# All heads of the second attention chunk score by two passes over exact halves

## The chip, the cores and the metric

The program runs on one core of one Trainium2 chip. Its time is device time in microseconds (us), the median of several runs. The core has a matrix engine (TensorE; PE in the profile, with its weight loads as PEld), a vector engine (VectorE, DVE), an activation engine (ScalarE, ACT), GpSimd (POOL) and a queue engine (SyncE, SP) that issues nearly all transfers. Each engine takes its own instructions in the order in which they are written down, and waits at an instruction until what it needs is there.

## The reference

The inputs are q, k and v (4 batches, 8 heads, 576 positions, 64 wide) and the weights of two feed-forward layers. All is float32.

```
scores = (q @ k^T) / sqrt(64)
scores = scores - slope[h] * |i - j|      where 0 <= i - j < 128, else -1e9
attn   = softmax(scores);  out = attn @ v
x  = out, heads side by side              # 2304 tokens x 512
x  = (silu(x @ w_gate) * (x @ w_val)) @ w_out        # 512 -> 1536 -> 512
h  = x @ w_in                                         # 512 -> 2048
y  = (h * tanh(softplus(h))) @ w_out2                 # 2048 -> 512
```

## The kernel before

The 2304 tokens are cut into five chunks (512, 384, 512, 512 and 384 tokens). For each chunk the kernel computes attention and then the first feed-forward layer; the second layer follows for all tokens. Chunk 0's attention stands alone at the start. From then on the two kinds of work are interleaved: while PE runs the feed-forward groups of one chunk, the attention of the next chunk is handed out in pieces between them. So the attention of the second chunk (chunk 1, the one that changes) lies among the feed-forward groups of chunk 0.

**Two ways to score a head.** `s_full(h)` (line 143) decides by the table `S_FULL` (line 28): in the first `S_FULL[ci]` pairs of heads of chunk `ci` the scores are plain float32 products, in the others they are made of halves. In the trace a plain product appears as `s_ps<-k,q`, two records per product. For the halves, `split` (line 190) makes three tiles of a head:

```
nc.scalar.activation(out=Q, in_=q, func=AF.Copy, scale=c)      # L203, ACT
hi_act(K1, k)                                                  # L123, ACT
nc.vector.scalar_tensor_tensor(out=Q[64:128], in0=q[64:128], ...)   # L205, DVE
lo_dve(KL, k, K1)                                              # L126, DVE
```

`Q` holds the rounded query on partitions 0 to 63 and what rounding left over on 64 to 127; `K1` holds the rounded key twice, `KL` its remainder twice. `score` (line 211) then runs two products per block, `s_ps<-K,Q` and `s_ps<-KL,Q`, with 128 instead of 64 rows of contraction. A plain pair needs one load of q and k for both heads (lines 165 and 166) and one scaling on ACT (L195). A head of halves needs its q and k twice, on both halves of the partitions (lines 173 and 174), and the scratch tiles `qraw`, `kraw`, `Q`, `K1` and `KL` exist once each, so that the load of one head waits for the split of the head before it.

**Scores of one head of chunk 1.** Its 384 tokens are four blocks of 64, 128, 128 and 64 queries, in two PSUM banks; each bank is one piece of work (`s_piece`, line 344), with a cost: 1.7 where the head is plain, 0.87 where it is made of halves. After the second bank the head is normalized (`norm`: L257, L260 on DVE, L264 on ACT), later transposed (`t_ps`, L271 on PE), masked on POOL and multiplied with v (`o_ps`).

**What sets the order.** PE's order is written out by hand: after each feed-forward group the loop hands out attention pieces until their share of the summed cost has caught up with the groups done. The order on DVE, ACT, POOL and SP is made by a scheduler when the kernel is built.

**What else DVE does there.** During chunk 0 the weights of the first layer arrive as 64-bit numbers and are converted: five steps on ACT and DVE (L434, L439, L446, L451, L460), then a split (`w<-cw,w`, L126). Feed-forward groups are `g_ps<-xt,w` (12 matmuls a group, 24 for one of twelve blocks) and `acc<-h,ringf` (8 records), with L686 on ACT and L687 and L697 on DVE behind them.

Of the kernel before, what the change touches and what calls it, by code (L numbers as in the profile page):

```python
# [24 lines left out]
PLAIN = 3  # L25
CT = DM // 128
A_CHUNKS = [512, 384, 512, 512, 384]
S_FULL = [4, 2, 0, 0, 0]
TB = 384
NPB = NT // (2 * TB)  # L30
NJ = NF2 // 2
# [62 lines left out]
def body(ctx: ExitStack, tc: tile.TileContext, qT, kT, vP, w1, w1o, w2, cst, yT):  # L94
# [903 lines left out]
    with tc.manual_schedule(engines={mybir.EngineType.PE}):  # L998
# [19 lines left out]
        bpool["a"] = ap0  # L1018
        atts = [attention(app, p, ci, S_FULL[ci], ci == 0) for ci, p in enumerate(plansA)]
        pieces = attention_pieces(atts)  # L1020
# [166 lines left out]
```

## Time and profile before

| | |
|---|---|
| median of 3 runs | 941.0 us (940.25 to 941.48) |
| the profiled execution's own time | 941.18 us |
| its span, first to last instruction | 939.4 us |
| busy: PE, PEld | 916.6 us (98%), 819.3 us (87%) |
| busy: DVE, ACT, POOL | 699.1 us (74%), 518.7 us (55%), 202.3 us (22%) |
| plain scores of chunk 1 | 32 records from 53.2 to 95.4 us |
| scores of chunk 1 from halves | 16 + 16 records from 109.8 to 144.1 us |

The profile is of one execution. Times in it count from the span's start. A row of the timeline gives the start, the duration, the engine, the line, the operation, the tiles (written <- read), a count, and in brackets how long the engine had stood idle and for whom. The end of a matmul is modelled, and neighbours overlap a little; the time from one start to the next start is the surer measure, on DVE and ACT too.

### The profile page before, as it was taken

What the parts mean: (1) busy time and instruction counts of PE and PEld (TensorE: products, weight loads), DVE (VectorE), ACT (ScalarE), POOL (GpSimd) and SP (SyncE); (2) the same over time, 40 slices, a digit from 0 to 9 for tenths busy, and PEclk for the clock granted to TensorE, in tenths of its full rate; (3) what the DMA queues carried; (4) which work ended last, traced back from release to release, by engine and by line L of the source; (5) the groups of instructions that cost most, each with busy time, mean ns of one, the idle gap of its engine ahead of it and who ended that gap; (6) DMA issues with size and microseconds to landing.
All of it is one profiled execution on the core that took longest, in us unless ns stands there. A gap on an engine that the chain in (4) does not pass through costs nothing. (4 is left out here: it accounts for less than half of the span.)

```text
span 939.4 us, 14535 instructions
## 1 busy us (share of the span) xinstructions
PE 916.6 (98%) x5016; PEld 819.3 (87%) x5016; DVE 699.1 (74%) x1333; ACT 518.7 (55%) x1127; POOL 202.3 (22%) x332
## 2 busy tenths in 40 slices
PE   5999999999999999999999999999999999999998
PEld 4755678899988888888888999999999999999998
DVE  6898996677866776477665896688976689766874
ACT  6765667666575755355433554555535646355442
POOL 1312132110310332001012455452013410121000
PEclk8899999999999999999999999999999999999999
DMA  9855433366646554164527986526793257930375
GB/s 347 269 242 173 153 117 106 102 220 201 198 112 192 184 181 153 32 208 156 162 97 267 382 292 210 224 85 209 250 300 119 68 191 259 301 122 3 105 260 196
DMA packets 76729, 174.86 MB, mean 186 GB/s; under 512 B 8944, under 2 KB 52336, under 8 KB 66928
## 3 DMA queue, kind: packets, MB, share of 16 engines
q1 hardware_dynamic: 76512, 173.67, 56.1%
q8 instruction: 40, 0.66, 0.3%
q14 instruction: 33, 0.27, 0.1%
q10 hardware_dynamic: 144, 0.26, 0.1%
HBM read 138.25 MB, written 35.65 MB: 185 GB/s over the span
## 5 line engine op out<-in xcount | busy, mean ns | idle before, releaser
L116 PE MATMUL g_ps<-xt,w 128*128 128x512 f32 (+1 forms) x1440 | 318.3, 373 | 0.0
L116 PEld LDWEIGHTS g_ps<-xt,w 128*128 128x128 f32 x1440 | 257.6, 188 | 36.7 <-issue 3.5
L116 PE MATMUL bk<-op,wout 128*128 128x384 f32 x1008 | 176.2, 334 | 2.1 <-DMA wout<-w2o 2.0
L116 PEld LDWEIGHTS bk<-op,wout 128*128 128x128 f32 x1008 | 174.7, 188 | 3.2 <-ACT op L123 1.6
L116 PE MATMUL bk<-xs,win 128*128 128x384 f32 x1008 | 175.8, 334 | 0.7 <-DVE G L759 0.5
L116 PEld LDWEIGHTS bk<-xs,win 128*128 128x128 f32 x1008 | 174.7, 188 | 1.4 <-DVE G L759 0.8
L116 PE MATMUL acc<-hh,ring 128*128 128x512 f32 (+1 forms) x432 | 132.3, 369 | 0.0
L123 ACT ACTIVATE op<-G 128x768 fp32r<-128x768 f32 x84 | 71.2, 848 | 64.1 <-PE bk L116 53.6
L280 POOL TENSOR_SCALAR_AFFINE_SELECT PT<-PT 128x256 f32<-128x256 f32 (+4 forms) x80 | 44.4, 570 | 230.3 <-ACT PT L277 230.1
L126 DVE TENSOR_TENSOR op<-G,op 128x768 fp32r<-128x768 f32 x84 | 80.0, 964 | 16.1 <-ACT op L123 15.4
L116 PEld LDWEIGHTS acc<-hh,ring 128*128 128x128 f32 x432 | 80.0, 188 | 9.8 <-ACT hh L123 0.4
L851 POOL TENSOR_TENSOR t<-w 128x256 f32<-128x256 f32 x48 | 42.0, 897 | 206.9 <-issue 110.7
L116 PE MATMUL acc<-hl,ring 128*128 128x512 f32 (+1 forms) x216 | 79.0, 366 | 0.0
L249 ACT ACTIVATE Pt<-Pt,sm 128x128 f32<-128x128 f32 (+1 forms) x160 | 62.6, 393 | 14.1 <-DVE sm L245 13.6
L759 DVE TENSOR_TENSOR G<-u,bk 128x384 f32<-128x384 f32 x72 | 39.7, 553 | 40.0 <-PE bk L116 38.5
L686 ACT ACTIVATE t<-g_ps 128x512 f32<-128x512 f32 (+1 forms) x60 | 32.9, 549 | 47.3 <-PE g_ps L116 47.3
L1131 ACT ACTIVATE G<-G 128x384 f32<-128x384 f32 x72 | 37.3, 518 | 37.4 <-DVE G L759 37.4
L123 ACT ACTIVATE hh<-t 128x512 fp32r<-128x512 f32 (+1 forms) x54 | 31.3, 579 | 44.4 <-DVE t L702 44.2
L687 DVE SCALAR_TENSOR_TENSOR t<-t,g_ps 128x512 f32<-128x512 f32 (+1 forms) x60 | 37.6, 628 | 23.2 <-ACT t L686 23.1
L264 ACT ACTIVATE Pt<-Pt,sm 128x128 f32<-128x128 f32 (+1 forms) x144 | 46.5, 393 | 9.8 <-DVE sm L260 9.5
L126 DVE TENSOR_TENSOR hl<-t,hh 128x512 fp32r<-128x512 f32 (+1 forms) x54 | 36.5, 677 | 16.0 <-ACT hh L123 15.2
L702 DVE SCALAR_TENSOR_TENSOR t<-t,g_ps 128x512 f32<-128x512 f32 (+1 forms) x54 | 33.7, 624 | 19.2 <-PE g_ps L116 18.0
(84 smaller groups left out, 1268.1 us busy)
## 6 DMA issues: line engine op xcount, KB each, us to landing
wout<-w2o SPq DMA_DIRECT2D x42, 1024.0 KB, 7.0
wraw<-w SPq DMA_DIRECT2D x16, 1024.0 KB, 5.3
w2o<-chl SPq DMA_DIRECT2D x16, 896.0 KB, 8.2
wst<-w SPq DMA_DIRECT2D x12, 1024.0 KB, 8.0
cw<-w1od SPq DMA_DIRECT2D x24, 512.0 KB, 4.5
w<-w2d SPq DMA_DIRECT2D x24, 512.0 KB, 3.5
w2d<-cw SPq DMA_DIRECT2D x16, 512.0 KB, 4.6
wraw<-w1o SPq DMA_DIRECT2D x6, 1024.0 KB, 6.8
```

The lines of the kernel that those rows point to most:

```text
L116: nc.tensor.matmul(out=out, lhsT=lhsT, rhs=rhs, start=start, stop=stop, skip_group_check=True)
L123: return nc.scalar.activation(out=out, in_=in_, func=AF.Copy)
L126: return nc.vector.tensor_tensor(out=out, in0=in_, in1=hi.bitcast(F32), op=ALU.subtract)
L249: last_of["sum"] = nc.scalar.activation(out=Pt[:q.qn], in_=Pt[:q.qn], func=AF.Exp, scale=-1.0, bias=sm[:q.qn, i:i + 1], accum_out=sm[:q.qn ...
L264: last_of["exp"] = nc.scalar.activation(out=pt, in_=pt, func=AF.Copy, scale=r)
L280: nc.gpsimd.affine_select(out=here, in_=prev, pattern=[[0, m], [1, n]], compare_op=ALU.is_ge, fill=0.0, base=0, channel_multiplier=-1,)
L686: tanhs.append(nc.scalar.activation(out=t[:, :n], in_=st["g"][:, :n], func=AF.Tanh, scale=0.5))
L687: nc.vector.scalar_tensor_tensor(out=t[:, :n], in0=t[:, :n], scalar=1.0, in1=st["g"][:, :n], op0=ALU.add, op1=ALU.mult)
L702: nc.vector.scalar_tensor_tensor(out=t[:, :n], in0=t[:, :n], scalar=0.5, in1=vps[:, :n], op0=ALU.mult, op1=ALU.mult)
L759: last_of["add"] = nc.vector.tensor_tensor(out=out, in0=a, in1=b, op=op)
L851: nc.gpsimd.tensor_tensor(out=x[:, o], in0=a, in1=b, op=ALU.subtract)
L1131: last_of["mish"] = nc.scalar.activation(out=out, in_=in_, func=AF.Mish)
```

## The change

The second entry of the table goes from 2 to 0. Heads 0 to 3 of chunk 1 are then loaded, split and scored as heads 4 to 7 are already.

```
-S_FULL = [4, 2, 0, 0, 0]
+S_FULL = [4, 0, 0, 0, 0]
```

Since the cost of their score pieces falls from 1.7 to 0.87, the pieces of chunk 1 are also handed out at other places. The first place is PE's order from the first scores of chunk 1 on (s_ps are scores, g_ps the gate and value products, o_ps attention times v, acc the output products). Before:

```order
L116 MATMUL s_ps<-k_389,q_388 128x256
L116 MATMUL s_ps<-k_389,q_388 64x192
L116 MATMUL g_ps<-xt,w 128x512 x6
L116 MATMUL s_ps<-k_389,q_388 64x192
L116 MATMUL s_ps<-k_389,q_388 128x128
L116 MATMUL g_ps<-xt,w 128x512 x6
L116 MATMUL s_ps<-k_389,q_388 128x256
L116 MATMUL s_ps<-k_389,q_388 64x192
L116 MATMUL g_ps<-xt,w 128x512 x12
```

The same place in the changed kernel, from the second bank of head 0 (K_453) to the first bank of head 1 (K_646) and what follows:

```order
L116 MATMUL s_ps<-K_453,Q 128x128
L116 MATMUL s_ps<-KL,Q 128x128
L116 MATMUL g_ps<-xt,w 128x512 x3
L116 MATMUL s_ps<-K_646,Q 128x256
L116 MATMUL s_ps<-KL,Q 128x256
L116 MATMUL s_ps<-K_646,Q 64x192
L116 MATMUL s_ps<-KL,Q 64x192
L116 MATMUL g_ps<-xt,w 128x512 x3
L116 MATMUL s_ps<-K_646,Q 64x192
L116 MATMUL s_ps<-KL,Q 64x192
L116 MATMUL s_ps<-K_646,Q 128x128
L116 MATMUL s_ps<-KL,Q 128x128
```

Between the two heads stood 6 g_ps, now there are 3; between the banks of head 1 stood 12, now there are 3; after head 1 come 12 g_ps, the transposes of head 0 and the scores of head 2.

The second place is DVE's order at the same time, from the first L687 of chunk 0 on. Before:

```order
L687 SCALAR_TENSOR_TENSOR t<-t,g_ps 128x512
L451 SCALAR_TENSOR_TENSOR cw<-wst,cw 128x1024
L238 COPY_PREDICATED s_ps<-cst_sb,s_ps 64x64 x2
L451 SCALAR_TENSOR_TENSOR cw<-wst,cw 128x1024
L687 SCALAR_TENSOR_TENSOR t<-t,g_ps 128x512
L697 SCALAR_TENSOR_TENSOR h<-t,g_ps 128x512
```

In the changed kernel (KL and Q are the remainders of head 1):

```order
L687 SCALAR_TENSOR_TENSOR t<-t,g_ps 128x512
L238 COPY_PREDICATED s_ps<-cst_sb,s_ps 64x64
L451 SCALAR_TENSOR_TENSOR cw<-wst,cw 128x1024
L245 ISA Pt,sm<-s_ps,cst_sb 128x128
L245 ISA sm 128x1
L245 ISA Pt,sm<-s_ps,cst_sb 64x128
L245 ISA sm 64x1
L126 TENSOR_TENSOR KL<-kraw,K_646 128x512
L205 SCALAR_TENSOR_TENSOR Q<-qraw,Q 64x384
L451 SCALAR_TENSOR_TENSOR cw<-wst,cw 128x1024
```

The split of head 1 stands behind the first L451 and two reductions of head 0; ahead of this piece DVE has the same instructions from the last `xt<-o_ps,xt` on as before.

The third place is ACT's order where head 0 is normalized (L264), in the changed kernel:

```order
L249 ACTIVATE Pt,sm<-Pt,sm 128x128
L123 ACTIVATE w<-cw 128x1024
L203 ACTIVATE Q<-qraw 128x384
L434 ACTIVATE cg<-wst 128x1024
L264 ACTIVATE Pt<-Pt,sm 64x128
L264 ACTIVATE Pt<-Pt,sm 128x128 x2
L264 ACTIVATE Pt<-Pt,sm 64x128
L123 ACTIVATE K_716<-kraw 128x512
```

Before, no split stood there:

```order
L123 ACTIVATE w<-cw 128x1024
L249 ACTIVATE Pt,sm<-Pt,sm 64x128
L249 ACTIVATE Pt,sm<-Pt,sm 128x128
L434 ACTIVATE cg<-wst 128x1024
L264 ACTIVATE Pt<-Pt,sm 64x128
L264 ACTIVATE Pt<-Pt,sm 128x128 x2
```

The rounding of head 2's queries now stands ahead of the normalization of head 0.

## Rows read from the trace of the kernel before

**Rows 1.** Stretches, us: length; PE, PEld, DVE, ACT, POOL busy (count); clock; DMA.

```profile
53.20:72.90 19.70, 17.51 (x65) 10.34 (x64) 18.99 (x47) 12.15 (x30) 0.17 (x1) 1.00 0.44 159
72.90:110.00 37.10, 37.10 (x151) 23.00 (x149) 34.24 (x67) 23.19 (x53) 9.32 (x22) 1.00 0.47 161
```

**Rows 2.** Waits of PE, 50 to 190 us: total, times, longest.

```profile
PE s_ps L116 <- DVE Q L205: 1.5, 2, 0.8
```

**Rows 3.** Timeline of PE, plain heads 0 to 2 of chunk 1.

```profile
53.18 1.16 PE L116 MATMUL s_ps<-k,q 64*128 64x256 f32 x4
54.27 1.83 PE L116 MATMUL g_ps<-xt,w 128*128 128x512 f32 x6
56.02 0.95 PE L116 MATMUL s_ps<-k,q 64*64 64x192 f32 x4
56.91 1.66 PE L116 MATMUL g_ps<-xt,w 128*128 128x512 f32 x6
...
63.69 0.92 PE L116 MATMUL s_ps<-k,q 64*64 64x192 f32 x4 [1.07 <-DVE sm L245]
...
72.14 0.89 PE L271 MATMUL t_ps<-cst_sb,Pt 128*128 128x128 f32 x4 [1.13 <-ACT Pt L264]
72.94 1.13 PE L116 MATMUL s_ps<-k,q 64*128 64x256 f32 x4
74.00 3.70 PE L116 MATMUL acc<-h,ringf 128*128 128x512 f32 x8
```

**Rows 4.** Timeline of PE, head 6 of chunk 1, from halves.

```profile
132.68 0.38 PE L116 MATMUL s_ps<-K,Q 128*128 128x256 f32 x1
...
133.20 2.94 PE L116 MATMUL g_ps<-xt,w 128*128 128x512 f32 x12
135.98 0.25 PE L116 MATMUL s_ps<-K,Q 128*64 128x192 f32 x1
...
136.35 2.97 PE L116 MATMUL g_ps<-xt,w 128*128 128x512 f32 x12
```

**Rows 5.** Timeline of DVE, from the last xt of chunk 0 on.

```profile
53.91 0.69 DVE L126 TENSOR_TENSOR xt<-o_ps,xt 128x512 fp32r<-128x512 f32 x1 [1.04 <-ACT xt L123]
...
57.39 0.68 DVE L687 SCALAR_TENSOR_TENSOR t<-t,g_ps 128x512 f32<-128x512 f32 x1
57.99 1.22 DVE L451 SCALAR_TENSOR_TENSOR cw<-wst,cw 128x1024 f32<-128x1024 uint32 x1
...
63.05 0.27 DVE L245 CUSTOM_DVE_ANT_0 Pt<-s_ps,cst_sb 128x128 f32<-128x128 f32 x1
...
95.92 0.68 DVE L126 TENSOR_TENSOR KL<-kraw,K 128x512 fp32r<-128x512 f32 x1
...
97.77 0.56 DVE L205 SCALAR_TENSOR_TENSOR Q<-qraw,Q 64x384 fp32r<-64x384 f32 x1
```

**Rows 6.** Timeline of ACT, conversion, normalization and split.

```profile
66.33 0.61 ACT L123 ACTIVATE K<-kraw 128x512 fp32r<-128x512 f32 x1
...
70.38 1.12 ACT L434 ACTIVATE cg<-wst 128x1024 bf16<-128x1024 bf16 x1
71.40 1.27 ACT L264 ACTIVATE Pt<-Pt,sm 64x128 f32<-64x128 f32 x4
...
95.69 0.52 ACT L203 ACTIVATE Q<-qraw 128x384 fp32r<-128x384 f32 x1 [0.32 <-PE s_ps L116]
```

**Rows 7.** Timeline of SP, the load of one head's queries.

```profile
98.43 2.51 SPq L173 DMA_DIRECT2D qraw<-qT  x4
```

**Rows 8.** Transfers 25 to 110 us: count, KB each, median us from issue to landing.

```profile
qraw<-qT SPq DMA_DIRECT2D x4, 80.0 KB, 2.4
```

**Rows 9.** Timeline of PE, the longest idle time after the start.

```profile
15.71 1.19 PE L271 MATMUL t_ps<-cst_sb,Pt 128*128 128x128 f32 x4 [3.01 <-ACT Pt L264]
```

**Rows 10.** Stretches of the first stage, columns as in rows 1.

```profile
16.00:18.00 2.00, 2.00 (x7) 1.48 (x7) 2.00 (x8) 2.00 (x5) 0.10 (x1) 0.50 1.10 410
...
30.00:32.00 2.00, 1.77 (x8) 1.22 (x8) 1.30 (x6) 2.00 (x8) 0.00 (x0) 1.00 0.85 277
```

## The prediction

> **What bounds the kernel now.** I read the summary page first. PE is busy in 98% of the span, so a microsecond taken off PE is worth up to a microsecond, provided that no wait comes in its place. Next I cut the stretch of the change out of the span. The plain scores of chunk 1 lie between 53.2 and 95.4 us, among the feed-forward groups of chunk 0. There PE and DVE are both nearly full: from 53.2 to 72.9 us DVE is busy for 18.99 of 19.70 us and PE for 17.51, from 72.9 to 110 us DVE for 34.24 of 37.10 us and PE for all of it [rows 1]. So two engines stand side by side at their limit, and the change moves work from one to the other. Then I read PE's timeline there, and its waits. PE waits twice with the plain heads, 1.07 us for a PSUM bank that DVE has yet to read and 1.13 us for the normalized rows of a head [rows 3]. With the heads made of halves that come later, it waits twice for L205, the remainder of the queries on DVE, 1.5 us together [rows 2]. That last wait is the one to ask about: heads 0 to 3 never have it now, and all eight can have it afterwards.
>
> **The saving on PE.** A plain head takes 1.09 us for its first bank (53.18 to 54.27) and 0.89 us for its second (56.02 to 56.91), together 1.98 us [rows 3]. A head made of halves takes 0.52 us (132.68 to 133.20) and 0.37 us (135.98 to 136.35), together 0.89 us [rows 4]. Four heads save 4 x 1.09 = 4.4 us of PE. This is a measured pair of the same shapes in the same chunk, so I hold it for safe to some 0.4 us.
>
> **What is added.** DVE gets a KL of 0.68 us and a Q of 0.56 us for each head [rows 5], 4 x 1.24 = 5.0 us. ACT gets a K of 0.61 and a Q of 0.52 us [rows 6] a head, 4.5 us, and loses two scalings of about the size of Q, so 3.5 us net. SP issues 8 transfers a head in place of 4 a pair, 24 more, at 2.51 / 4 = 0.63 us each [rows 7]: 15 us of SP, which nothing on PE's path waits for directly. The bytes double to 0.46 MB a head; DMA has a share of 0.44 there [rows 1], so I take nothing for it. What counts is when the halves of each head are there.
>
> **The walk through the first three heads.** PE's order puts the first bank of head 1 behind only three g_ps. PE starts head 0 at 53.18 as before: its halves come from loads that stand early in SP's queue, and they lie beside chunk 0's own attention. The first bank ends at 53.7. The six g_ps need the last xt of DVE (53.91 + 0.69 = 54.6 [rows 5]) and end at about 56.0, at 0.25 us each (2.97 us for twelve [rows 4]). Second bank 0.37, three g_ps 0.75: at 57.1 PE stands at head 1.
>
> DVE does the same as before up to its first L451, which runs from 57.99 to 59.21. Behind it now stand two reductions of 0.27, KL with 0.68 and Q with 0.56 us [rows 5]: 61.0 by the listed durations, 60.9 with the small overlap of neighbours. **PE waits 3.8 us** (57.1 to 60.9). What is queued behind the waiting score is all of PE's work, above all the first groups of the next weight block.
>
> From 60.9 PE does 0.52 + 0.75 + 0.37 + 2.97 = 4.6 us (head 1 with three g_ps, then twelve), to 65.5. Next are the transposes of head 0 and the scores of head 2. Two chains lead there. First, ACT: kraw and qraw exist once, so SP can issue head 2's load only when DVE has read head 1's, at 60.9. The last of the query transfers is the seventh of eight, issued 6 x 0.63 = 3.8 us later [rows 7], landing 2.4 us after that [rows 8], at 67.1. ACT's Q stands ahead of a conversion step and of head 0's normalization, so 67.1 + 0.52 + 1.12 + 1.27 = 70.0 [rows 6] for the last of head 0's normalized rows. Second, DVE: between Q of head 1 and KL of head 2 it has four instructions like L451 (1.22 each), four of about 0.65 like L687, some thirteen small ones of 0.1 to 0.35, and Q and KL themselves. That is 11.8 us by listed durations and about 10 with full overlap of neighbours; I take 10.8, so 71.7. PE has 0.8 us of transposes (72.14 to 72.94 [rows 3]) and a first pass of about 0.25 us to do meanwhile. **PE waits 71.7 - 65.5 - 1.05 = 5.1 us** more. The stretch has 3.8 + 5.1 = 8.9 us of waiting where it had 1.07 + 1.13 = 2.2 us [rows 3]: 6.7 us more.
>
> From head 3 on the pieces lie 8 to 15 us apart, with at least a group of acc (3.7 us [rows 3]) and twelve g_ps between heads. A load with its split takes about 3.8 + 0.63 + 2.4 + 0.61 + 0.52 + 1.24 = 9.2 us, so most heads are ready; I leave the waits there at the 1.5 us of rows 2, with bounds of 1.5 us less and 3 us more. The five steps of weight conversion lose DVE time early too, but no wait of PE for a converted weight shows among its waits in this stretch, and I take 0.
>
> **The clock.** A wait of 3.8 us is longer than any that PE has after the start. The longest now is 3.01 us, up to 15.71 [rows 9], and right behind it the granted clock is 0.50, 1.2 GHz, at 16 to 18 us; by 30 to 32 us it is back at 1.00, 2.4 GHz [rows 10]. If the clock falls at 60.9, the 4.6 us of work there take up to 9.2, which is mostly hidden under the wait for head 2; what is still slow after 71.7 costs. The ends are 0 (it stays, or is back by then) and about +3 (low for another 6 us of work, at half speed). I take +1.
>
> **The sum.** -4.4 + 6.7 + 1.0 = +3.3 us on the profiled execution's 941.2 gives 944.5. That execution stands 0.2 us above the median of 941.0, so I predict **944.3 us** as a median, slower. No later stage gives it back: PE is busy nearly without a gap afterwards, and it takes its work in order.
>
> **A rule that weighs the engines otherwise.** In the stretch from 53.2 to 72.9 us the weight loads are busy for 10.34 of 19.70 us, 52%, where DVE has 96% [rows 1]. The Trainium skill (Perfetto Trace Analysis, Identifying the Most-Contended Engine) says that the busy share of matmuls is a poor measure of how near TensorE is to its limit, that weight-load share is the better one, and that the engine with the highest share is the one to relieve. By that rule DVE is the engine that bounds this stretch, and the change loads it further; the trace agrees in so far as PE's waits there end on DVE or behind it. It gives the second rival below.
>
> **The rivals.**
> - *PE's saving stands.* One mechanism: the halves of heads 1 and 2 are in time, because DVE and ACT get to them sooner than the walk says. For it: PE never waited more than 0.8 us for halves of heads 4 to 7 [rows 2]. Against it: those heads have 12 or more g_ps around them, head 1 has three. It decides at 57.1 us: if Q of head 1 is done by then, the first wait is gone, and with it most of the second. Time: 941.0 - 4.4 = 936.6, up to 939 with one of the small waits left.
> - *DVE is the bound of the whole stretch.* Then PE's saving is worth nothing, and the end of the stretch moves by what DVE gets beyond its free time: its idle time from 53.2 to 110 us is 0.71 + 2.86 = 3.6 us [rows 1], and it gets 5.0. That is +1.4 us, 942.4, about no change. Against it: DVE's work is not all needed by PE at once, so neither the full price nor the full cover need show.
> - *More goes wrong than I count.* The clock falls and stays low beyond head 2 (+3 in place of +1), and the loads of heads 3 and 5 come late (+3): 949.
> - *The scores don't become cheaper.* Excluded by rows 3 and 4, which show both forms in this chunk.
>
> **How the numbers follow.** A measurement of this kernel can tell a change of 0.2%, 1.9 us, from none. I give the forecast 0.50, with a range of its own from 942 to 947.5; the saving that stands 0.16; DVE as the bound, or early waits that just eat the saving, 0.22; more gone wrong 0.12. A small part of the forecast's own range, 0.04, lies within 0.2%. So faster 0.16, same 0.26, slower 0.58. The range of 938 to 949 leaves out about a half of the first rival and a half of the last.
>
> **What would show each step.** The scores of heads 0 to 3, now 16 records with K and 16 with KL, should take about 0.9 us a head. PE should show an idle time near 4 us before the first score of head 1, released by L205 or by KL, and another 2 to 4 us each before the transposes of head 0 and before the scores of head 2. The granted clock from 61 to 75 us shows the clock term. DVE should have no idle time between 54 and 72 us. I am wrong if PE's wait before head 1 is under 1.5 us, or if heads 4 to 7 show waits of several us that the walk doesn't have.

## The result: slower by 1.0%, and the profile after

The changed kernel took **951.0 us** as a median (948.55 to 953.31, four runs), the kernel before 941.2 us beside it: a ratio of 1.0098, 95% interval 1.0071 to 1.0125. A second set, timed later, gave 950.3 us and 1.0111 (1.0093 to 1.0130). The prediction of 944.3 us had the direction and about a third of the size, and its range ended at 949. The profiled execution took 948.55 us with a span of 946.7, 7.3 us more than the span before; this is the difference that the two traces can explain line by line.

I cut it at PE's first score of chunk 1 and at the start of a later weight block that both kernels have. The first score starts at 56.05 us where it was 53.18 [rows 3]: **2.9 us are lost before the changed scores begin.** The later block starts at 144.19 us before, and at 152.86 after, less 1.25 us for one o_ps that the changed kernel does ahead of it: 91.0 us from the first score before, 95.6 after: **4.6 us are lost in the stretch of the change.** Together 7.4 with rounding. The two starts of the later block:

```profile
144.19 2.98 PE L116 MATMUL g_ps<-xt,w 128*128 128x512 f32 x12
152.86 5.66 PE L116 MATMUL g_ps<-xt,w 128*128 128x512 f32 x24
```

The first loss is in chunk 0's own attention. Timeline of PE of the changed kernel (start, duration, instruction, count, and in brackets the idle time before it with what ended it):

```profile
34.82 0.62 PE L116 MATMUL o_ps<-PT,qkv 128*64 128x256 f32 x2 [0.70 <-POOL sm L216]
36.57 3.14 PE L116 MATMUL o_ps<-PT,qkv 128*64 128x256 f32 x14 [1.14 <-POOL PT L284]
...
56.05 0.39 PE L116 MATMUL s_ps<-K,Q 128*128 128x256 f32 x1
```

ACT's timeline there:

```profile
32.06 0.51 ACT L203 ACTIVATE Q<-qraw 128x384 fp32r<-128x384 f32 x1
32.48 0.62 ACT L123 ACTIVATE K<-kraw 128x512 fp32r<-128x512 f32 x1
...
33.76 0.69 ACT L264 ACTIVATE Pt<-Pt,sm 128x128 f32<-128x128 f32 x2
34.35 0.58 ACT L277 ACTIVATE PT<-t_ps 128x512 f32<-128x512 f32 x1
```

And the same copy in the kernel before:

```profile
33.06 0.60 ACT L277 ACTIVATE PT<-t_ps 128x512 f32<-128x512 f32 x1 [0.34 <-POOL PT L280]
```

Head 0's split (L203 and L123) stands among the exponentials, and the copy of the transposed rows (L277), which stood ahead of all four exponentials of a head, now stands behind two of them and a normalization (L264). The copy is 1.3 us later, POOL masks it later, and the 16 o_ps that PE ran without a gap are broken by waits of 0.70 and 1.14 us. In this execution the 14 behind the second wait then run at half clock (3.14 us; a second profile below has 1.73).

The second loss begins as the walk said. Timeline of PE from the three g_ps behind head 0's second bank to head 2:

```profile
59.34 0.92 PE L116 MATMUL g_ps<-xt,w 128*128 128x512 f32 x3
63.98 0.58 PE L116 MATMUL s_ps<-K,Q 128*128 128x256 f32 x1 [3.72 <-DVE Q L205]
...
66.92 4.49 PE L116 MATMUL g_ps<-xt,w 128*128 128x512 f32 x12
72.07 0.89 PE L271 MATMUL t_ps<-cst_sb,Pt 128*128 128x128 f32 x4 [0.66 <-ACT Pt L264]
73.31 0.36 PE L116 MATMUL s_ps<-K,Q 128*128 128x256 f32 x1 [0.34 <-DVE Q L205]
74.87 0.39 PE L116 MATMUL s_ps<-KL,Q 128*128 128x256 f32 x1 [1.21 <-DVE KL L126]
```

DVE's timeline over the same wait:

```profile
61.10 1.21 DVE L451 SCALAR_TENSOR_TENSOR cw<-wst,cw 128x1024 f32<-128x1024 uint32 x1
...
62.66 0.68 DVE L126 TENSOR_TENSOR KL<-kraw,K 128x512 fp32r<-128x512 f32 x1
63.37 0.56 DVE L205 SCALAR_TENSOR_TENSOR Q<-qraw,Q 64x384 fp32r<-64x384 f32 x1
```

PE waits 3.72 us for head 1 (predicted 3.8), released by exactly the instruction that was named, two reductions and KL behind L451. It stands at acc behind head 2's first bank 19.2 us after its first score (75.27 less 56.05; the walk gives 18.7). The twelve g_ps at 66.92 take 4.49 us, not 2.97 [rows 4]: the clock is low there, and the waits before head 2 are 0.66 + 0.34 + 1.21 = 2.2 us, not the 5.1 of the walk. Stretches of the changed kernel (length, busy time of PE, PEld, DVE, ACT and POOL with counts, granted clock, DMA), which answer to [rows 1]:

```profile
56.05:75.27 19.22, 12.80 (x50) 9.31 (x49) 18.38 (x46) 11.94 (x29) 0.58 (x3) 0.82 0.32 113
75.27:112.40 37.13, 35.94 (x158) 23.62 (x156) 33.52 (x77) 23.75 (x68) 12.13 (x20) 1.00 0.51 167
```

PE is busy for 4.7 us less in the first stretch (12.80 of 19.22, 17.51 of 19.70 before); DVE is as full as it was. Waits of PE from 28 to 200 us, which answer to [rows 2] (total, times, longest):

```profile
PE s_ps L116 <- DVE Q L205: 7.0, 4, 3.7
PE o_ps L116 <- POOL PT L284: 1.4, 2, 1.1
PE s_ps L116 <- DVE KL L126: 1.2, 1, 1.2
PE o_ps L116 <- POOL sm L216: 0.7, 1, 0.7
```

The 7.0 us are 3.72 and 0.34 as above, and two later waits of 1.69 us (head 5, at 112.89) and 1.27 us (head 7, at 142.16): 2.96 where [rows 2] has 1.5.

### The profile page after: what moved, and what is told of

The parts are those of the page before. It is cut to its first block, busy times and chain, and to the rows that moved or that the text cites. A ratio compares the mean times of both kernels' runs of the same rounds, so it can differ in the third digit from the quotient of the medians.

```text
span 946.7 us, 14595 instructions
## 1 busy us (share of the span) xinstructions
PE 917.8 (97%) x5016; PEld 822.9 (87%) x5016; DVE 704.9 (74%) x1341; ACT 520.6 (55%) x1133; POOL 206.5 (22%) x332
## 5 line engine op out<-in xcount | busy, mean ns | idle before, releaser
L123 ACT ACTIVATE op<-G 128x768 fp32r<-128x768 f32 x84 | 71.1, 847 | 64.1 <-PE bk L116 53.6
L280 POOL TENSOR_SCALAR_AFFINE_SELECT PT<-PT 128x256 f32<-128x256 f32 (+4 forms) x80 | 42.9, 550 | 219.3 <-ACT PT L277 219.1
L123 ACT ACTIVATE hh<-t 128x512 fp32r<-128x512 f32 (+1 forms) x54 | 31.2, 578 | 49.2 <-DVE t L702 49.0
L687 DVE SCALAR_TENSOR_TENSOR t<-t,g_ps 128x512 f32<-128x512 f32 (+1 forms) x60 | 37.6, 626 | 25.5 <-ACT t L686 25.4
L264 ACT ACTIVATE Pt<-Pt,sm 128x128 f32<-128x128 f32 (+1 forms) x144 | 46.3, 390 | 15.1 <-DVE sm L260 14.8
L284 POOL TENSOR_SCALAR_AFFINE_SELECT PT<-PT 128x256 f32<-128x256 f32 (+4 forms) x80 | 48.6, 625 | 1.6
```

The costliest lines, as they stand in the source:

```text
L123: return nc.scalar.activation(out=out, in_=in_, func=AF.Copy)
L264: last_of["exp"] = nc.scalar.activation(out=pt, in_=pt, func=AF.Copy, scale=r)
L280: nc.gpsimd.affine_select(out=here, in_=prev, pattern=[[0, m], [1, n]], compare_op=ALU.is_ge, fill=0.0, base=0, channel_multiplier=-1,)
L284: nc.gpsimd.affine_select(out=prev, in_=prev, pattern=[[0, m], [-1, n]], compare_op=ALU.is_gt, fill=0.0, base=0, channel_multiplier=1,)
L687: nc.vector.scalar_tensor_tensor(out=t[:, :n], in0=t[:, :n], scalar=1.0, in1=st["g"][:, :n], op0=ALU.add, op1=ALU.mult)
```

## Experiments

Theory 1 was that the loss is made by waits: head 0's split inside chunk 0's attention, head 1's scores too close behind head 0, and the low clock after the idle time. All ratios are to the kernel before, timed beside each kernel, with 95% intervals.

### Places or halves

First the halves at the old places, and the new places without halves:

```
- return (a.ci, 1.7 if a.s_full(h) else 0.87, f)
+ return (a.ci, 1.7 if a.s_full(h) or (a.ci == 1 and h < 4) else 0.87, f)   # old costs
+ return (a.ci, 1.7 if a.ci == 0 else 0.87, f)       # new places, S_FULL = [4, 2, 0, 0, 0]
```

> The halves of the change, but heads 0 to 3 of chunk 1 keep the cost of 1.7 in PE's planner, so that their pieces stay where the kernel before has them (six groups of the feed-forward between head 0 and head 1, not three). Theory 1 (the loss is made by places: 2.9 us from head 0's split inside chunk 0's attention, 3.7 us before head 1, then the low clock): the wait before head 1 shrinks to about 3.7 - 0.75 - some of the second bank = 2.5 us or less, the rest stays: 944 to 948 us. Rival A (DVE's added 5 us bound the stretch wherever the pieces stand): 951, as the change. Rival B (only the dense places cost): 937 to 939, since PE's saving of 4.4 us is then all that is left.

Measured: 944.4 us, 1.0037 (1.0019 to 1.0055). The places alone take back two thirds of the loss; rival A falls, rival B too.

> The plain products of the kernel before, at the places of the change (cost 0.87 for all heads of chunk 1, so three groups between head 0 and head 1). Theory 1: a plain head needs no split on DVE, so denser places alone cost only what comes of PE being 0.75 us sooner at a bank: 941 to 943 us. Rival B (dense places alone cost): 945 to 951, with waits before head 1 on the bank that DVE has yet to read. The clock should stay at 1.00 from 60 to 75 us by theory 1.

Measured: **950.8 us, 1.0110** (1.0077 to 1.0143). Theory 1 expected 941 to 943 and falls here: plain products, which need no split, lose as much at the new places as the change does. PE's timeline of this kernel:

```profile
51.93 1.16 PE L116 MATMUL s_ps<-k,q 64*128 64x256 f32 x4
...
62.57 5.08 PE L116 MATMUL g_ps<-xt,w 128*128 128x512 f32 x12 [3.10 <-DVE sm L245]
70.87 1.17 PE L271 MATMUL t_ps<-cst_sb,Pt 128*128 128x128 f32 x4 [3.22 <-ACT Pt L264]
71.84 1.99 PE L116 MATMUL s_ps<-k,q 64*128 64x256 f32 x4
73.77 5.45 PE L116 MATMUL acc<-h,ringf 128*128 128x512 f32 x8
...
155.10 5.66 PE L116 MATMUL g_ps<-xt,w 128*128 128x512 f32 x24
```

The waits have other releasers, a bank that DVE's reductions have yet to read (L245) and the normalized rows, but similar lengths and places: 3.10 and 3.22 us, against 3.72 and 2.2. Whoever comes this early waits for DVE, halves or not.

The equal totals hide two different sums. The first score stands at 51.93 here, so nothing is lost ahead of it. The same two cuts as above (again less 1.25 us) give 101.9 us from the first score to the later block, 10.9 more than before. PE's waits account for 5.3 of that (3.10, 3.22, and 1.56 and 1.14 at heads 5 and 7, less the 3.7 of before). The matmuls at low clock behind the first two waits account for about 5.4, an estimate from the starts of like matmuls. The halves at the old places have these two starts:

```profile
54.35 0.39 PE L116 MATMUL s_ps<-K,Q 128*128 128x256 f32 x1
...
144.77 2.98 PE L116 MATMUL g_ps<-xt,w 128*128 128x512 f32 x12
```

That is 90.4 us (here nothing is to be taken off, since PE's order is that of before). So in this stretch plain products take 91.0 us at the old places and 101.9 at the new, halves 90.4 and 95.6. The places cost in both forms. The halves gain 6 us at the new places and nothing clear at the old, where waits eat what PE saves; the loss ahead of the stretch is theirs alone. These are single executions, those of the three altered kernels 1.4 to 2.6 us under their medians.

DVE's work is spread otherwise afterwards, too. The stretch from 76 to 88 us of the kernel before,

```profile
76.00:88.00 12.00, 12.00 (x44) 7.20 (x44) 10.23 (x19) 6.31 (x13) 0.20 (x2) 1.00 0.37 132
```

of the new places with plain products,

```profile
76.00:88.00 12.00, 12.00 (x38) 5.97 (x36) 2.55 (x9) 2.78 (x11) 1.68 (x7) 0.95 0.00 1
```

and of the changed kernel:

```profile
76.00:88.00 12.00, 12.00 (x46) 7.39 (x45) 9.04 (x26) 7.15 (x26) 5.88 (x12) 1.00 0.51 157
```

With the plain heads pulled forward, PE first waits behind DVE, and then has feed-forward work left with which DVE has little to do (2.55 of 12 us). In the change the stretch holds 9.04, not far from the 10.23 before. What the empty stretch costs by itself is not shown. I call this theory 2: places decide, because they set how PE's and DVE's work overlap.

Next, half of the change, `S_FULL = [4, 1, 0, 0, 0]`, at the new costs and at the old:

> Half of the change: heads 0 and 1 of chunk 1 plain, heads 2 and 3 by halves. Theory 1: no split inside chunk 0's attention and none between head 0 and head 1, so the 2.9 and the 3.7 us and the fall of the clock go; PE saves 2 x 1.09 = 2.2 us and pays perhaps 1 to 2 us of waits before head 2: 939 to 942 us. Rival A (DVE's volume bounds): half of the loss, 945 to 946.

Measured: 940.9 us, 1.0002 (0.9982 to 1.0022).

> Only heads 2 and 3 by halves, with the old cost of 1.7 for both pairs, so every piece stays where the kernel before has it. PE saves 2 x 1.09 = 2.2 us, DVE gets 2.5 us, nothing changes before 62 us. Theory 2 (places decide): 938 to 939.5, faster than the kernel before by 0.1 to 0.2%, and faster than one pair at the new costs (940.9). Rival (volume of DVE): no gain, 940 to 941.

Measured: 941.3 us, 1.0012 (0.9992 to 1.0032). No gain at either cost, and no loss: for heads 2 and 3 the place does not matter while heads 0 and 1 stay plain at the old places. That points to heads 0 and 1 for what the places lose; no run puts these two alone at dense places. Theory 2's hope for a gain fails: at the old costs PE's waits for Q (0.61 at head 5, 2.00 at head 7), before head 2 (1.76) and at head 1 (1.08) make 5.5 us, where the same places had 3.7 [rows 2, 3]. That takes 1.8 of the 2.2 us saved.

Then still sparser places, cost 2.6 for heads 0 to 3:

> The halves of the change with cost 2.6 for heads 0 to 3 of chunk 1: 15 groups between head 0 and head 1 where the change has 3 and the kernel before 6, and more work before head 2. Theory 2 (places decide; the halves themselves are a gain): PE comes to head 1 some 3 us later than in the change, about when Q is ready, so the wait before head 1 is 0 to 1 us, PE's clock stays, and the time is 939 to 942 us (the loss inside chunk 0's attention, 1.2 to 2.4 us, is still there). Rival (DVE's added 5 us bound the stretch): the waits only move behind later heads, and the time is that of the old costs, 944 to 945.

Measured: 943.2 us, 1.0037 (1.0018 to 1.0056), no better than the old costs. PE's timeline:

```profile
59.96 3.65 PE L116 MATMUL g_ps<-xt,w 128*128 128x512 f32 x15
66.24 0.39 PE L116 MATMUL s_ps<-K,Q 128*128 128x256 f32 x1 [2.63 <-DVE Q L205]
```

PE comes 3.65 us after head 0's second bank and still waits 2.63 us. In DVE's row a second L687, a second L451 and an L697 (0.67, 1.21 and 0.67 us, at 62.59 to 64.99) stand ahead of KL and Q there: more groups between the heads bring their own DVE work, and so their own delay.

### The loss inside chunk 0's attention

```
- run(k + 1, "split")
+ with tc.issue_after(last_of["sum"].ins) if k + 1 == H else ExitStack():   # late split
+     run(k + 1, "split")
+ with tc.high_priority(500) if ci == 0 else ExitStack():                   # copies first (L277)
```

The late split alone, on the change:

> The change, with the split of chunk 1's head 0 held back until the last sums of chunk 0's attention are done, nothing else. Theory 1: the 2.9 us that chunk 0's attention lost come back, as far as head 0's halves are still there at about 53 us (they have some 15 us): 948 us as a median, and the span up to the first score of chunk 1 is about 53.2 us again, with PE's wait before head 1 as it was (3.7 us). Rival: the 2.9 us is not from the split but from a different order of POOL's and ACT's work that the change makes anyway: 951, first score at 56.

Measured: 948.1 us, 1.0079 (1.0055 to 1.0103), the time that theory 1 gave, and in part for its reason. PE's timeline:

```profile
35.76 3.14 PE L116 MATMUL o_ps<-PT,qkv 128*64 128x256 f32 x14 [1.49 <-POOL PT L284]
...
54.43 0.39 PE L116 MATMUL s_ps<-K,Q 128*128 128x256 f32 x1
```

The first score comes 1.6 us sooner than in the change (1.2 counted from PE's first matmul, at 5.74 and 6.18 us), with the 14 o_ps equally slow in both. But they still wait 1.49 us for POOL: ACT's copy is still behind the normalization, though the split is gone from there. So the place of the split is one part of the loss, and the order of the copies is the other. Both edits, with the old costs:

> The halves at the old costs (as in the first experiment), with head 0's split held back behind chunk 0's last sums and ACT's copies of chunk 0's transposed rows put ahead of its normalizations. It tests the loss inside chunk 0's attention. Theory: ACT's order there, not its load, makes PE wait for POOL's masked rows; with the copies earlier the wait before the 14 o_ps (1.14 us) shrinks to about 0.5 and the first score of chunk 1 comes 0.6 to 1.2 us sooner: 943.4 as a median against 944.4. Rival: it is the load of the split (1.1 us of ACT), and all of it comes back: 942.

Measured: 941.2 us, 1.0007 (0.9988 to 1.0027), against 1.0037 without them: 0.3% or 2.8 us back. PE's timeline:

```profile
35.47 1.73 PE L116 MATMUL o_ps<-PT,qkv 128*64 128x256 f32 x14 [0.18 <-POOL PT L285]
...
52.73 0.39 PE L116 MATMUL s_ps<-K,Q 128*128 128x256 f32 x1
```

The wait is 0.18, not 1.14 us, and the first score stands at 52.73; with the old costs alone it was 54.35. PE still waits 3.03 us for head 1 there (at 61.07), so the 4.4 us saved on PE do not show. Both edits on the change itself:

> The change at its own dense places, with head 0's split behind chunk 0's last sums and ACT's copies of chunk 0 early: the cure that took the old-cost version from 944.4 to 941.2. If the two losses add: 951.0 - 3.2 = 947.8 (and first score of chunk 1 near 53, o_ps wait under 0.3 us). If chunk 0's loss is hidden behind DVE at the dense places: 950 to 951.

Measured: 949.0 us, 1.0082 (1.0063 to 1.0101). First score at 53.11, wait 0.19, as they should be, yet only some 0.2% of the two sets of the change (1.0098, 1.0111) comes back, and the intervals overlap. Whether less comes back here than the 2.8 us at the old places is therefore not shown. The trace has one place where a part goes: PE waits 1.89 us for head 0's rows, 0.66 in the change.

### The low clock

14 matmuls that nobody needs fill PE's wait before head 1, and in a second kernel 15 more the one before head 0's transposes:

```
+ if ci == 1 and h == 1 and g == 0:                 # score(h, g), ahead of the products
+     for _ in range(14):
+         mm(s_ps, wt[1][:, 0, :128], x_t[0][:, 0, 0, :512], True, True)
+ if ci == 1 and h == 0:                            # transp(h): 15 into t_ps, second kernel only
```

> The change, and 14 more matmuls of 128x512 (about 0.22 us each, 3.1 us) into the bank of head 1's scores just before them; the real product overwrites them. They fill PE's wait of 3.7 us, so the granted clock should be 1.00 from 62 to 72 us where it was 0.50. Theory 'the low clock costs by itself': the 4.6 us of work that took 7.0 comes back, about -2.4 us, 948.5, and the runs scatter less. Rival 'DVE holds the place anyway': PE only arrives earlier at the transposes of head 0 and at head 2 and waits there for the same instructions of ACT and DVE, so the waits before head 2 grow from 2.2 to 4 or 5 us and the time stays at 951.

Measured: 955.3 us, 1.0155 (1.0123 to 1.0188), slower than either side expected.

> The change with PE's two long idle times filled: 14 matmuls of 128x512 before head 1's scores as in the fill before, and 15 more before the transposes of head 0, both overwritten by the real products. With the first fill alone the granted clock was 0.50 to 0.80 from 72 to 80 us, behind a wait of 3.64 us, with DVE idle for 4.7 us at 80 to 88. If the low clock costs there: the clock is 1.00 from 58 to 84 us, and the time 3 to 4 us below the single fill's 955, 951 to 952. If it costs nothing: 955. If both waits' low clocks are what the change loses to its places: below 949.

Measured: 949.2 us, 1.0086 (1.0068 to 1.0103). PE's timeline with one wait filled,

```profile
71.90 0.89 PE L274 MATMUL t_ps<-cst_sb,Pt 128*128 128x128 f32 x4 [3.64 <-ACT Pt L267]
...
75.85 5.70 PE L116 MATMUL acc<-h,ringf 128*128 128x512 f32 x8
```

and with both:

```profile
72.59 0.89 PE L277 MATMUL t_ps<-cst_sb,Pt 128*128 128x128 f32 x4 [0.31 <-ACT Pt L267]
...
76.15 3.62 PE L116 MATMUL acc<-h,ringf 128*128 128x512 f32 x8
```

One fill keeps the clock at 1.00 from 56 to 72 us and wins nothing: PE only comes earlier to the next wait, which grows from 0.66 to 3.64 us, and the clock falls behind that one, where nothing covers it (8 acc in 5.70, not 3.62 us). With both filled the clock stays up from 56 to 112 us. 6 us come back against the single fill, but only 1 to 2 against the change, whose intervals overlap with this one. So the low clock at 64 to 71 us was mostly covered in the change by the wait for head 2, as the prediction supposed, and without it some 8 us of loss remain. That is not the loss without any low clock: at 36 to 40 us this profile has 0.58 and at 116 to 120 us 0.68.

### DVE's volume

Theory 3 took DVE's added work itself as the price. I added it to the kernel before, with nothing taken from PE:

```
+ with tc.issue_after(last_of["max"].ins):       # heads 1 to 3 of chunk 1; nobody reads pad
+     nc.vector.tensor_tensor(out=pad, in0=k, in1=k, op=ALU.subtract)
+     nc.vector.scalar_tensor_tensor(out=pad[64:128, :p.n], in0=q[64:128], scalar=c, ...)
```

> The kernel before with DVE work added and nothing taken from PE: for heads 1 to 3 of chunk 1 a subtraction of 128x512 and one of 64x384 into a spare tile that nobody reads, each behind DVE's last reduction of the head before it: 3 x 1.24 = 3.7 us of DVE. Theory 3 (from 54 to 112 us DVE is the limit; before has some 4 us of DVE idle there in all): slower by 1 to 4 us, 941.5 to 944. Theory 2 (only PE's places and its waits for halves count): nothing waits for the added work, 940 to 940.5.

Measured: 941.4 us, 1.0008 (0.9991 to 1.0025). 3.7 us of DVE cost 0.8 us by the ratio (1.8 by the medians, 941.4 and 939.6), and the interval holds no difference too. Volume alone is not the price of the change. Then the other way round, KL on POOL (in the kernel before this is heads 4 to 7, which are made of halves there):

```
- lo_dve(KL, k, K1)
+ nc.gpsimd.tensor_tensor(out=KL, in0=k, in1=K1.bitcast(F32), op=ALU.subtract)   # chunk 1
```

> The kernel before with the remainder of the keys of heads 4 to 7 of chunk 1 computed on POOL, not on DVE: 4 x 0.68 = 2.7 us less on DVE, on an engine that is busy 9 of 37 us there. Theory 3: up to 2.7 us faster, 937.5 to 939.5, if POOL is not much slower at it. Theory 2: no change, 940, or slower where POOL is late with it.

Measured: 942.0 us, 1.0023 (1.0007 to 1.0040): slower.

> The change (all of it, at its own dense places) with the remainders of the keys of chunk 1 on POOL: 0.68 us less of DVE before each head's scores, 5.4 us less over the chunk. Theory 3: the wait before head 1 shrinks from 3.7 to about 3, the ones before head 2 by about 1.4, and the time falls by 2 to 4 us, 947 to 949. Theory 2: the places stay bad, 950 to 951.

Measured: 949.7 us, 1.0106 (1.0086 to 1.0126): no change against the two sets of the change. Theory 3 had forecast 941.5 to 944 with the added work, a gain in the kernel before, and 947 to 949 here. It misses the first and the last narrowly, and the second has the wrong sign. The last test is at the old places, with the late split, the early copies and all eight KL on POOL:

> The halves at the old places, with head 0's split late, chunk 0's copies early, and the remainders of the keys of chunk 1 on POOL. Theory 3: what DVE is relieved of (5.4 us over the chunk, about 3 of it before 112 us) comes back nearly whole from 941.2: 937 to 939, faster than the kernel before. Theory 2: PE's waits for Q stay, 940.5 to 941.5.

Measured: **938.2 us, 0.9979** (0.9960 to 0.9998). Here theory 3 is right with its 937 to 939, and theory 2 is wrong with 940.5 to 941.5: in this set the work taken off DVE comes back (1.0007 without it).

> Old places, late split, copies early, the remainder of the keys of chunk 1 on POOL, unaltered. If the gain is real: ratio 0.996 to 0.9995. If it was a lucky set of executions: 1.000 to 1.002, as its sibling with POOL for four heads.

Measured again: 939.2 us, 0.9988 (0.9976 to 1.0001). It is the fastest version of this study, by 1 to 2 us, at the edge of what can be told from no change; by this second set the gain over 1.0007 is not clear either. The stretch that was empty of DVE's work in the plain products at the new places is full in it (11.94 of 12 us):

```profile
76.00:88.00 12.00, 12.00 (x50) 7.96 (x49) 11.94 (x26) 7.54 (x18) 4.21 (x6) 1.00 0.48 159
```

Two siblings, KL on POOL for heads 0 to 3 only, and that with cost 2.6:

> Old places, late split, copies early, and the remainder of the keys on POOL for heads 0 to 3 only (heads 4 to 7 on DVE as in the kernel before, where moving them to POOL cost 0.23%). If POOL's later remainders are what costs there: 936 to 937.5, faster than with all eight on POOL (938.2) and than the kernel before by 0.3%. If the relief of DVE is what gains: 938.5 to 940.

Measured: 943.6 us, 1.0019 (1.0004 to 1.0033); a miss. In its profiled execution the 14 o_ps of chunk 0 take 3.19 us at a low clock behind a wait of 0.91, where the version above has 1.73 behind 0.29.

> The same with cost 2.6 for heads 0 to 3, so 15 groups between head 0 and head 1. If PE's wait before head 1 (2.8 us at the old places) is what is left of the loss: it shrinks to 1 us or less and the time falls by 1 to 2 us against the run beside it. If DVE's share holds the place: the same as the run beside it, since head 1's queries come behind more of DVE's work for those groups, as in the sparse run before (Q at 66.2 us).

Measured: 942.4 us, 1.0011 (1.0001 to 1.0022). Why the remainders of all eight heads on POOL are better than those of heads 0 to 3 alone, and those of heads 4 to 7 worse than none in the kernel before, I have not settled. So how much DVE's volume counts at the old places stays open.

### The change a second time

> The change itself, once more, unaltered. If its runs scatter because the granted clock falls in some executions and not in others after waits of 1 to 2 us (at 108 to 114 us and at 34 to 36 us), this profile shows other stretches of low clock than the first, at the same waits, and its time differs from 948.55 by about half the length of those stretches. Median 949 to 951.5, ratio to the kernel before 1.009 to 1.011.

Measured: 950.3 us, 1.0111 (1.0093 to 1.0130); this profiled execution took 947.38. Stretches of the first profile,

```profile
36.00:40.00 4.00, 3.43 (x17) 2.07 (x18) 1.20 (x8) 1.72 (x7) 0.62 (x2) 0.57 0.66 170
64.00:68.00 4.00, 4.00 (x14) 3.41 (x15) 4.00 (x9) 0.91 (x5) 0.00 (x0) 0.50 0.24 57
112.00:116.00 4.00, 3.11 (x16) 2.64 (x17) 3.94 (x7) 3.09 (x7) 3.01 (x6) 1.00 0.73 283
```

and of the second:

```profile
36.00:40.00 4.00, 3.88 (x26) 2.88 (x26) 2.33 (x12) 3.12 (x13) 0.26 (x3) 1.00 0.47 122
64.00:68.00 4.00, 4.00 (x13) 3.22 (x12) 4.00 (x14) 1.93 (x5) 0.00 (x0) 0.50 0.37 102
112.00:116.00 4.00, 4.00 (x12) 3.07 (x11) 4.00 (x6) 1.89 (x5) 1.89 (x4) 0.57 0.46 135
```

Behind the waits at 36 and at 112 us the clock (the third column from the right) fell in one execution and not in the other. The 14 o_ps took 3.14 and 1.73 us, the 12 g_ps behind head 5's wait 2.95 and 4.53. Head 5's wait is 1.69 us in both. The o_ps wait 1.14 us in both, but only in the first execution had PE idled another 0.70 us just before. So such a wait can cost another 1.4 to 1.6 us; the one before head 7 (1.27 and 1.16 us) did so in neither. PE's timeline of the second profile:

```profile
36.12 1.73 PE L116 MATMUL o_ps<-PT,qkv 128*64 128x256 f32 x14 [1.14 <-POOL PT L284]
...
54.19 0.39 PE L116 MATMUL s_ps<-K,Q 128*128 128x256 f32 x1
```

The first score stands at 54.19, not 56.05: here only 1.0 us is lost ahead of it (1.5 counted from PE's first matmul). The other 1.4 of the 2.9 us was the low clock behind the wait.

## Why the prediction was wrong

**The waits of heads 1 and 2: right in sum.** 3.72 us for 3.8, and 19.2 us to acc behind head 2's first bank for 18.7, with the releasers that the walk named. The second wait is 2.2 us for 5.1; 2.8 us of slow matmuls stand in the rest of it, as the term for the clock allowed. From the first score on, the sum said +3.3 us and the profiled execution shows +4.6: 4.4 saved, 5.6 more of waits, 2.8 of low clock, and 0.6 that I cannot place. The saving on PE was right too: a head's scores take 0.9 us where nothing waits and the clock is up.

**The step that failed first: "they lie beside chunk 0's own attention", taken at nothing.** It measured +2.9 us in the first profile and +1.0 in the second, which has no low clock there. I looked at where head 0's loads stand in SP's queue, and not at what its split displaces on ACT; the planned order on ACT, POOL and DVE from 30 to 37 us was there to be read. The two edits of ACT's order give back 2.8 us at the old places, and 1.5 to 2.7 us at the change's own (1.0098 or 1.0111 less 1.0082, with overlapping intervals). Of the 6.7 us from 944.3 to 951.0 this step is 2.9, the stretch from the first score on 1.3 (the later heads), and 2.5 lie between the profiled execution and the median.

**The later heads: too small.** "I leave the waits there at 1.5 us" measured 2.96, inside the bounds that I gave.

**The clock: half right.** At 64 to 71 us it cost 2.8 us of PE's time (63.98 to 71.41, so 7.4 for the 4.6 of the walk), and the fills show that most of this was hidden. What I had no term for is the clock behind the short waits, 1.4 us at 36 to 40 us in one execution and 1.6 at 112 to 116 in the other.

**The cause behind the walk: wrong in part.** I put the waits down to the halves, which must be ready where plain heads have none to wait for. The new places with plain products lose 10 us without a split. The walk got its number because it followed DVE's order, and PE at these places waits for DVE's order whatever stands in it.

**DVE as the bound: the right engine, not the right price.** The rival with DVE's volume as the bound (+1.4 us) names the engine on which PE's waits end. So does the Trainium skill (Perfetto Trace Analysis, Identifying the Most-Contended Engine), by which the engine with the highest occupancy is the one to optimize first. The trace agrees: DVE is busy for 18.38 of 19.22 us in the first stretch, and PE's 3.72 us at head 1 end on it. But 3.7 us more on DVE cost 0.8 us by the ratio, and 2.7 us less on it, with POOL doing the work, made the kernel before 0.2% slower.

**Still open.** In both sets of the change the profiled execution is the fastest, 2.5 and 2.9 us under the median. Different falls of the clock can account for such a spread, but no trace shows one of the longer executions, so this part of the 9.8 us is not shown. The mean granted clock on record fits it: 0.994 or 0.995 in the three of the nine under 949 us, 0.980 to 0.992 in the six above 950. It is no proof, since this record can miss a fall (see below). That the new places of heads 0 to 3 lose is shown, 6 us with halves and 10 with plain products; which single piece among them does it is not.

## What to carry to other kernels

Where two engines are full side by side and a planner places work by its cost, a cheaper piece can change the order on both: look where the planner puts it now, and try the new places with the old work before you blame the work. When two variants lose the same in all, cut both traces at the same points before you call the causes the same. Walk the first stretch after a change, but also the one before it, since an order made by a scheduler can shift ahead of the edit, and count for each new wait of PE the slow clock that may follow. A stretch in which the second full engine has little to do, behind one where the first waits for it, can be a mark of work that was pulled too far forward; it was plain with the plain products here, and faint in the change itself.

## What the runs showed of the hardware

- The granted clock falls after an idle time in some executions and not in others of the same program: behind 1.69 us before head 5, twelve g_ps took 2.95 us in one and 4.53 in the other.
- The clock's row can miss a fall. At 16 to 18 us the change's profile says 1.00 and that of before 0.50 [rows 10], but the eight s_ps from 16.8 us take 3.35 us in both, and eight like them 1.78 us at 32 us. Durations are the safer reading.
- POOL took 1.26 to 3.33 us for the subtraction of 128x512 for which DVE takes 0.68 [rows 5].
